# Masks of two half batches by GpSimd, their decay by one product a block, gates on SP's queue, and a new order of the work

## The chip, the cores and the metric

The kernel runs on one core of a Trainium2 chip. The time is device microseconds of one execution, as a median over runs. The engines of the core are TensorE (PE, with its weight loads PEld), VectorE (DVE), ScalarE (ACT), GpSimd (POOL) and SyncE (SP), which only issues transfers; ScalarE can issue transfers too. The transfers themselves run on 16 DMA engines that all queues share.

## The reference

Attention with a decay (a forget gate `f` for each key), then a gated FFN with a convolution of three taps. Shapes: 8 batches, 8 heads, 576 positions, 64 numbers a head; the FFN is 512 -> 1024 -> 512.

```python
scores = scale * np.matmul(q, k.transpose(0, 1, 3, 2))
cum = np.cumsum(np.log(np.clip(f, 0.0001, 1.0)), axis=-1)
decay = cum[:, :, :, None] - cum[:, :, None, :]
scores = np.where(causal, -1000000000.0, scores + decay)
attn = softmax(scores)
x = heads side by side of (attn @ v)
...
h = np.maximum(x @ w_in, 0.0)
conv_out = sum of three taps: conv_w[k] * h moved by k - 1 positions
out = (h * (1 / (1 + np.exp(-conv_out)))) @ w_out
```

## The kernel before

**Half batches.** Attention is worked off in 16 half batches `hb` of four heads, each as two pairs of heads (`i` = 2 hb + pair). Keys stand on the partitions and queries on the columns, so a score tile is a transposed block. For each half batch TensorE makes the blocks on the diagonal (`sd{i}`, 1024 columns, two heads), the blocks beside it (`so{i}.{s}`, 1024 columns, one head), and the last 64 positions of four heads (`st{hb}`, 256 columns); ScalarE takes the exponential of each (`ed`, `eo`, `et`) out of one of four PSUM tiles into fp16. Then TensorE multiplies with v (`pv{hb}.0`, `pv{hb}.1`), VectorE divides by the sums (`n`, `m`), the result is turned (`t`, `tx`), and batch b's FFN runs in eight pieces: product `f{b}.{ff}`, relu `r` on ScalarE, convolution `c` and `d` on VectorE, tanh `a` on ScalarE, gate `g` on VectorE, second product `o`, copy-out `e`, store `s`.

**Loads.** For half batches 0 and 1, q and k are loaded plainly (`ld`, L159), turned on TensorE (`tp`, L166) and copied out of PSUM with a change of the lower halves of the numbers (`cl`, L172 on ScalarE, L174 on VectorE): a float32 is read as two 16-bit rows, the upper halves are the bf16 number, and the rows of lower halves are free for other use. All other half batches are loaded with a DMA transpose (`q{hb}.{side}`, L180), from half batch 4 on into the tiles that the half batch four before it has left. v is loaded in five pieces a batch (`v{b}.{kb}`, L211, two tiles) and cast to fp16 (`va{hb}.0`, `va{hb}.1`, L219 and L221); the FFN's weights are loaded in four pieces each (`wi`, `wo`, L516) and cast (`wic`, `woc`, L524).

**Decay.** `dca` clips the gates, `dcl` takes the logarithm, `dcs` the running sum, `dck` splits it into two bf16 rows a head (`kc`, upper and lower part on partitions 0 to 63 and 64 to 127), and `ki` (L279) writes them to DRAM (`image`). The free rows of q and k then carry the decay through the same product as the scores: half batches 1 to 7 get theirs by two small row transfers (`rw{hb}`, L204 and L205), half batches 8 to 15 by a fill from `image` and a block of zeros (`fi{hb}`, L195 and L197), which also waits for `zc` (L282 to L285). Half batch 0 has no row transfer; there each block gets two further products (L315 with `sel_k`, L317 with `sel_q`).

**Causal mask.** With `MASK_PE` naming all of half batches 0 to 7, TensorE first writes the mask to a diagonal or tail tile with a product of its own (L320). For half batches 8 to 15 the exponential goes to float32 (`pd`, `p3`), and GpSimd clears the masked half on its way to fp16 (`md`, `mt`, L356 and L335).

**Order.** `ORDER` lists every step by hand; each engine, and each queue of transfers, works off its own steps in that order, and steps with a choice of engine have it behind an `@`. `add` names what a step waits for (`after`), which of a fixed number of buffers it takes and frees (`take`, `give`). The steps of SP's queue up to the second fill, in order:

```
ld0.0.0 ld0.1.0 ld0.0.1 v0.0 ld0.1.1 ld1.0.1 ld1.0.0 v0.1 v0.2 v0.3 v0.4 ki q2.1 q2.0 wi1 rw1 wi0 wi2 wi3 rw2
q3.0 q3.1 q4.1 v1.0 v1.4 v1.1 rw3 v1.3 v1.2 q4.0 q5.0 q5.1 wo3 wo1 wo0 v2.0 v2.3 v2.4 v2.1 v2.2 wo2
q6.0 q6.1 q7.0 q7.1 v3.0 v3.1 rw6 v3.2 zc v3.3 v3.4 rw7 q9.1 q8.1 q9.0 q8.0 fi9 fi8
```

The gates `f` and `conv_w` go by ScalarE's queue (L224, L226), and so do `rw4` and `rw5`.

Of the kernel before, what the change touches and what calls it, by code (L numbers as in the profile page):

```python
# [56 lines left out]
def kernel(  # L57
# [142 lines left out]
    def rows_of(hb, e="SP"):  # L200
        dma = {"SP": nc.sync, "ACT": nc.scalar}[e].dma_start
        h0 = 2 * PAIRS if hb == 0 else 0
# [1 line left out]
        dma(even_rows(hb, 0, 1, h0 * S, HS), image[0:1, 0, c, :].rearrange("j h s -> j (h s)"))  # L204
# [495 lines left out]
```

## Time and profile before

| | us |
|---|---|
| median of the runs shown (3) | 244.96 |
| lowest, highest | 244.57, 245.11 |
| the profiled execution | 244.36 |
| its span | 242.6 |

| engine | busy us | share of the span |
|---|---|---|
| TensorE | 227.2 | 94% |
| ScalarE | 207.2 | 85% |
| VectorE | 205.3 | 85% |
| GpSimd | 51.0 | 21% |

The span runs from the first to the last instruction of one profiled execution; what lies around it belongs to the time too. Busy times of different engines overlap, and matmuls are pipelined, so a single matmul's duration is longer than the step from one to the next; the chain of waits shows the steps. In a row, `out<-in` names tiles, `xN` counts instructions, and the bracket behind a timeline row tells how long the engine was idle before it and what ended that.

### The profile page before, as it was taken

What the parts mean: (1) busy time and instruction counts of PE and PEld (TensorE: products, weight loads), DVE (VectorE), ACT (ScalarE), POOL (GpSimd) and SP (SyncE); (2) the same over time, 40 slices, a digit from 0 to 9 for tenths busy, and PEclk for the clock granted to TensorE, in tenths of its full rate; (3) what the DMA queues carried; (4) which work ended last, traced back from release to release, by engine and by line L of the source; (5) the groups of instructions that cost most, each with busy time, mean ns of one, the idle gap of its engine ahead of it and who ended that gap; (6) DMA issues with size and microseconds to landing.
All of it is one profiled execution on the core that took longest, in us unless ns stands there. A gap on an engine that the chain in (4) does not pass through costs nothing.

```text
span 242.6 us, 6390 instructions
## 1 busy us (share of the span) xinstructions
PE 227.2 (94%) x2627; PEld 145.6 (60%) x2627; DVE 205.3 (85%) x324; ACT 207.2 (85%) x278; POOL 51.0 (21%) x77
## 2 busy tenths in 40 slices
...
GB/s 203 328 201 236 279 187 232 176 246 279 200 196 217 196 136 237 199 293 207 219 240 286 207 185 277 272 116 191 249 206 215 220 194 4 125 177 58 173 86 218
DMA packets 120344, 49.53 MB, mean 204 GB/s; under 512 B 109863, under 2 KB 110631, under 8 KB 120315
## 3 DMA queue, kind: packets, MB, share of 16 engines
...
HBM read 20.97 MB, written 10.17 MB: 128 GB/s over the span
## 4 chain that ended last, share of the span: by engine, by line
PE 80%; DMA 6%; DVE 5%; SPq 4%; ACT 3%; issue 1%; ACTq 0%; DVEq 0%
PE ps L474 24%; PE ps L429 21%; PE ps L312 15%; PE ps L389 7%; SPq L180 3%; PE ps L394 3%; DMA qk<-in_q_dram 3%; PE ps L166 2%; PE ps L320 2%; PE ps L414 2%; DMA qk<-image 2%; DMA pd<-in_moe_conv_w_dram 2%; PE ps L315 1%; PE ps L317 1%; DVE u L446 1%; ACT pp L370 1%
## 5 line engine op out<-in xcount | busy, mean ns | idle before, releaser
L429 PE MATMUL ps<-xt,w_in_f 128*128 128x512 f16 (+1 forms) x512 | 70.1, 286 | 0.4 <-DVE xt L417 0.4
L370 ACT ACTIVATE pp<-ps 128x1024 f16<-128x1024 f32 x64 | 64.6, 1030 | 3.5 <-PE ps L312 2.1
L474 PE MATMUL ps<-w_out_f,hg 128*128 128x512 f16 x288 | 66.7, 379 | 0.0
L312 PE MATMUL ps<-qk 128*128 128x128 bf16 (+2 forms) x576 | 63.7, 240 | 2.1 <-DMA qk<-image 1.0
L446 DVE SCALAR_TENSOR_TENSOR u<-ht,cwt 128x576 f32<-128x576 f16 x64 | 52.9, 841 | 4.4 <-ACT ht L440 4.3
L451 ACT ACTIVATE hg<-u,cw 128x576 f16<-128x576 f32 x64 | 48.6, 781 | 6.1 <-DVE u L448 6.0
L448 DVE SCALAR_TENSOR_TENSOR u<-ht,cwt,u 128x576 f32<-128x576 f16 x64 | 53.3, 846 | 0.5
L429 PEld LDWEIGHTS <-w_in_f 128*128 128x128 f16 x512 | 34.3, 98 | 28.8 <-issue 0.5
L312 PEld LDWEIGHTS <-qk 128*128 128x128 bf16 x576 | 39.4, 98 | 19.9 <-issue 4.2
L440 ACT ACTIVATE ht<-ps 128x576 f16<-128x576 f32 x64 | 40.9, 661 | 6.3 <-PE ps L429 2.8
L474 PEld LDWEIGHTS <-hg 128*128 128x128 f16 x288 | 26.9, 98 | 28.9
L458 DVE SCALAR_TENSOR_TENSOR hg<-hg,ht 128x576 f16<-128x576 f16 x51 | 38.6, 767 | 0.6 <-ACT hg L451 0.5
L356 POOL TENSOR_SCALAR_AFFINE_SELECT pp<-pd 128x1024 f16<-128x1024 f32 x16 | 19.7, 1245 | 54.0 <-ACT pd L353 54.0
L389 PE MATMUL ps<-va,pp 128*128 128x65 f16 x640 | 24.8, 193 | 1.7 <-DVE va L219 1.7
L389 PEld LDWEIGHTS <-pp 128*128 128x128 f16 x640 | 22.5, 97 | 4.2 <-DVE va L219 2.0
L405 DVE TENSOR_TENSOR xm<-ps,rc 128x896 f16<-128x896 f32 (+1 forms) x32 | 23.9, 751 | 0.5
L353 ACT ACTIVATE pp<-ps 128x1024 f16<-128x1024 f32 x16 | 16.5, 1034 | 4.8 <-PE ps L312 3.3
L353 ACT ACTIVATE pd<-ps 128x1024 f32<-128x1024 f32 x16 | 16.3, 1022 | 2.3 <-PE ps L312 1.6
L219 POOL CAST va<-vf 128x1024 f16<-128x1024 f32 x8 | 9.8, 1228 | 31.1 <-DVE xm L405 18.5
L320 PE MATMUL ps<-mask,ident 128*128 128x512 bf16 (+1 forms) x40 | 14.5, 365 | 1.3 <-ACT pp L370 0.8
L403 DVE RECIPROCAL rc<-ps 128x14 f32<-128x14 f32 (+1 forms) x32 | 6.7, 209 | 9.5 <-PE ps L394 5.8
L479 ACT COPY ob<-ps 128x1024 f32<-128x1024 f32 (+1 forms) x14 | 12.8, 918 | 0.3 <-issue 0.2
...
## 6 DMA issues: line engine op xcount, KB each, us to landing
vf<-in_v_dram SPq DMA_DIRECT2D x32, 256.0 KB
...
out_dram<-ob SPq DMA_DIRECT2D x3, 256.0 KB
```

The source lines that it names most:

```text
L312: nc.tensor.matmul(o, tk[:, h * S + k0:h * S + k0 + 128], tq[:, h * S + q0:h * S + q0 + n], start=first, stop=last and not by_matmul(hb, h))
L353: nc.scalar.activation(o, ps_of(f"sd{i}").rearrange("p (s c) -> p s c", s=2), AF.Exp, scale=SCALE)
L370: nc.scalar.activation(pair(i)[:, s, 512:1536], ps_of(f"so{i}.{s}"), AF.Exp, scale=SCALE)
L389: nc.tensor.matmul(ps[:, c:c + D + 1], block(hb, h, m, n), va[:, h, m, 0:D + 1], start=(m == 0), stop=(m == n))
L405: nc.vector.tensor_tensor(xm[:, CUT * D * u:CUT * D * u + nj * k * D].rearrange("p (j x d) -> p j x d", x=k, d=D), got[:, :, :, 0:D], r.un ...
L429: nc.tensor.matmul(ps[:, t0:t1], w_in_f16[:, cc, 128 * ff:128 * (ff + 1)], xt[:, cc // 2, x:x + t1 - t0], start=(cc == 0), stop=(cc == NCC ...
L440: nc.scalar.activation(ht_of(b, ff)[:, 2:2 + S], ps_of(f"f{b}.{ff}")[:, 0:S], AF.Relu, scale=1.0 if (b, ff) in LATE else 0.5)
L446: nc.vector.scalar_tensor_tensor(u, ht[:, 1:1 + S], cwt[:, ff, 0:1], ht[:, 2:2 + S], op0=ALU.mult, op1=ALU.add)
L448: nc.vector.scalar_tensor_tensor(u, ht[:, 3:3 + S], cwt[:, ff, 1:2], u, op0=ALU.mult, op1=ALU.add)
L451: nc.scalar.activation(hg_of(b, ff), u_t[slot[f"c{b}.{ff}", "u"]], AF.Sigmoid if (b, ff) in LATE else AF.Tanh, scale=cw[:, ff, 1:2])
L458: nc.vector.scalar_tensor_tensor(hv, hv, 1.0, ht_of(b, ff)[:, 2:2 + S], op0=ALU.add, op1=ALU.mult)
L474: nc.tensor.matmul(ps[:, 512 * j:512 * (j + 1)], w, w_out_f16[:, ff, :], start=(ff == 0), stop=(ff == NFF - 1))
```

## The change

`MASK_PE` loses half batches 0 and 1: their masks go to GpSimd as `md0` to `md3`, `mt0`, `mt1`. `PAIRS` becomes `DIRECT = 2`: for half batches 0 and 1, each block gets one further product, of a key row block `row_k` for its head with `row_q`. `row_q` holds minus the scaled running sums of batch 0's eight heads on partitions 32 to 39 (`dcq`, on POOL) and ones elsewhere; `row_k` of a head is `kc` with all rows but its own two cleared and -1 in the row of its queries (`dk0` to `dk7`, on VectorE, one for each head). `rw1` is gone. The `row_k` lie in the last two `pp` tiles and `row_q` in the last `xt` tile until these are first used; `hix` and `hfx` lie in what becomes a float32 tile of the tails.

The gates are loaded by SP (`fl`), behind `wi1`, which is now the very first transfer. Part of the constants become steps of the order: `un` (L246 and L250 of before), `zv` (clearing of `va` and `ht`), `zm` (the rows for `zc`, behind the masks since they lie in `pd`). Two exponential steps wait for `cw` or `un`, in whose buffers they write.

The order is made anew throughout, and with it the engine of 47 steps: among others the casts of `w_in` go to POOL (two), ScalarE and VectorE (one each) instead of POOL (four), those of `w_out` to VectorE instead of POOL, `va1` from POOL to VectorE; `rw4` and `rw5` go by SP, `rw3`, `rw6` and `rw7` by ScalarE. SP's steps up to the second fill are now:

```
wi1 fl ld0.0.0 ld0.0.1 ld0.1.0 ld1.0.0 ld0.1.1 ld1.0.1 v0.0 q2.0 q2.1 ki v0.2 v0.1 v0.3 v0.4 rw2 wi2 q3.0 wi0 q3.1 wi3
v1.0 v1.3 v1.1 v1.2 v1.4 q4.1 q4.0 q5.0 q5.1 v3.0 rw4 wo1 wo2 v2.0 rw5 v2.1 v2.3 wo0 wo3 q6.0 v2.2 v3.1
q6.1 q7.1 v2.4 q7.0 zc v3.3 v3.2 v4.0 q9.1 q8.1 v3.4 q8.0 v4.2 q9.0 fi8 fi9
```

TensorE's first steps are now `tp0.0.0 tp0.0.1 cw tp0.1.0 tp1.0.0 tp0.1.1 sd0` (before: `cw tp0.0.0 tp0.0.1 tp0.1.0 tp0.1.1 sd0`), and around the fills `f2.7 so14.0 o1.0 pv7.0 st7 sd16 pv7.1 o1.1 sd18` (before: `o1.1 sd18 pv7.0 sd16 pv7.1 sd19 t6 f2.7`).

```diff
-    PAIRS = 2
+    DIRECT = 2
-    MASK_PE = (0, 1, 2, 3, 4, 5, 6, 7,)
+    MASK_PE = (2, 3, 4, 5, 6, 7,)
...
+    index = cpool.tile([128, HH, SL], FP32, name="index")
+    hix, hfx = index[:, 0:2].rearrange("p h j -> p (h j)").bitcast(I32), index[:, 2:4].rearrange("p h j -> p (h j)")
+    pick = cpool.tile([128, 8], FP32, name="pick")
+    sign = cpool.tile([128, 8], FP32, name="sign")
...
+    row_k = [pp_t[NP - 1 - h // 4].bitcast(BF16).rearrange("p s c -> p (s c)")[:, 768 * (h % 4):768 * (h % 4) + 640]
+             for h in range(DIRECT * HH)]
+    row_q = xt_t[NXT - 1].bitcast(BF16)[:, 0, 0:S]
...
-    nc.scalar.dma_start(fsb, f.rearrange("b h s -> (b h) s"))
+    def load_gates():
+        nc.sync.dma_start(fsb, f.rearrange("b h s -> (b h) s"))
...
+    nc.vector.tensor_scalar(pick, hfx[:, 0:8], lit[:, 2:3], None, op0=ALU.is_equal)
+    nc.vector.tensor_scalar(sign, hfx[:, 32:40], lit[:, 0:1], -1.0, op0=ALU.is_equal, op1=ALU.mult)
...
+    def decay_q(e):
+        if e == "ACT":
+            nc.scalar.activation(row_q[32:40], cum[0:8], AF.Copy, scale=float(-1.0 / SCALE))
+        else:
+            {"POOL": nc.gpsimd, "DVE": nc.vector}[e].tensor_scalar(row_q[32:40], cum[0:8], float(-1.0 / SCALE), None, op0=ALU.mult)
+
+    def decay_k(h):
+        nc.vector.tensor_scalar(row_k[h][:, 0:S], kc, pick[:, h:h + 1], sign[:, h:h + 1], op0=ALU.mult, op1=ALU.add)
...
-        if by_matmul(hb, h):
-            nc.tensor.matmul(o[0:m], kc[:, k0:k0 + m], sel_k[:, h:h + 1].broadcast_to((128, n)),
-                             start=False, stop=False)
-            nc.tensor.matmul(o, sel_q[:, h, :], kc[:, q0:q0 + n], start=False, stop=last)
+        if own:
+            nc.tensor.matmul(o, row_k[HH * hb + h][:, k0:k0 + 128], row_q[:, q0:q0 + n], start=False, stop=last)
...
-        nc.tensor.matmul(o, ident, mask[:, 0:j].unsqueeze(1).broadcast_to((128, n, j)), start=True, stop=False)
+        nc.tensor.matmul(o, ident_b, mask[:, 0:j].unsqueeze(1).broadcast_to((128, n, j)), start=True, stop=False)
...
+    add("fl", "SP", [], load_gates)
+    add("un", "DVE", [], units)
+    early = [x for x in range(2) if x not in MASK_PE]
+    add("zm", "POOL", [f"md{2 * x + p}" for x in early for p in range(2)], levels)
+    add("zv", "POOL", [], pads)
+    add("zc", "SP", ["zm"], constants)
+    add("dca", "DVE", ["fl"], lambda: nc.vector.tensor_scalar(fsb, fsb, 1e-4, 1.0, op0=ALU.max, op1=ALU.min))
...
+    add("dcq", "POOL/ACT/DVE", ["dcs"], decay_q)
+    for h in range(DIRECT * HH):
+        add(f"dk{h}", "DVE", ["dck"], lambda h=h: decay_k(h))
...
-            if hb == 0:
-                ready = [["dck"] + [f"cl0.{p}.{side}" for side in range(2)] for p in range(2)]
+            if hb < DIRECT:
+                ready = [["dcq"] + [f"dk{HH * hb + 2 * p + s}" for s in range(2)] + [f"cl{hb}.{p}.{side}" for side in range(2)]
+                         for p in range(2)]
```

More of the change, by code (lines that the diff above doesn't have):

```diff
@@ new lines @@
+wi1 ld0 fl ld0.0.0 tp0.0.0 ld0.0.1 dca dcl dcs un dck cl0.0.0@ACT tp0.0.1 dk0 dk1 cw ld0.1.0 cwt cl0.0.1@ACT dk2 zv
+ld1 ld1.0.0 dcq@POOL tp0.1.0 dct cl0.1.0@ACT tp1.0.0 ld0.1.1 cl1.0.0@DVE tp0.1.1 dk3 cl0.1.1@ACT ld1.0.1 dk4 sd0 ed0
+tp1.0.1 tp1.1.0 v0.0 sd1 q2.0 ed1 md0 cl1.1.0@DVE so1.1 eo1.1 md1 dk7 so0.0 tp1.1.1 eo0.0 dk5 q2.1 so1.0 cl1.0.1@DVE
+so0.1 ki cl1.1.1@DVE eo1.0 v0.2 sd2 dk6 so2.1 eo0.1 st1 eo2.1 v0.1 so2.0 et1 cl2.1 v0.3 ed2 cl2.0 mt1 va0.0@POOL sd3
+st0 ed3 eo2.0 so3.1 et0 v0.4 so3.0 rw2@SP eo3.1 eo3.0 wi2 sd4 so4.0 pv0.0 md2 md3 sd5 n0.0 m0.0 q3.0 wi0 wic2@POOL mt0
@@ new lines @@
+va0.1@ACT ed5 ed4 va1.0@DVE q3.1 pv0.1 va1.1@DVE pv1.0 n0.1 wi3 pv1.1 n1.0 m0.1 m1.0 eo4.0 n1.1 t0 wic0@POOL m1.1 v1.0
+so5.1 t1 tx0@DVE wic1@ACT v1.3 tx1@DVE cl3.0 so4.1 cl3.1 v1.1 eo4.1 so5.0 eo5.1 f0.0 wic3@DVE eo5.0 r0.0 v1.2 f0.1
+r0.1 c0.0 c0.1 f0.2 f0.3 d0.0 rw3@ACT st2 h0 r0.2 et2 r0.3 f0.4 c0.2 va2.0@DVE v1.4 f0.5 r0.4 a0.0 va2.1@ACT d0.2 g0.0
+pv2.0 pv2.1 va3.0@ACT c0.4 r0.5 n2.0 st3 a0.2 d0.4 m2.0 et3 a0.4 sd6 q4.1 cl4.1 n2.1 ed6 sd7 ed7 c0.3 so7.1 c0.5 so6.0
+m2.1 q4.0 g0.2 zm eo7.1 d0.3 so6.1 so7.0 f0.6 q5.0 cl4.0 d0.5 eo6.1 eo6.0 eo7.0 q5.1 va3.1@ACT d0.1 f0.7 g0.4 pv3.0
@@ new lines @@
+v3.0 a0.5 rw4@SP cl5.0 n3.0 r0.7 a0.3 wo1 pv3.1 n3.1 t2 wo2 m3.0 v2.0 cl5.1 r0.6 m3.1 a0.1 rw5@SP c0.7 tx2@ACT sd9 t3
+tx3@DVE ed9 d0.7 g0.5 sd8 v2.1 c0.6 v2.3 f1.0 f1.1 ed8 a0.7 g0.7 g0.1 r1.0 so9.1 woc2@DVE d0.6 woc1@DVE f1.2 so9.0
+eo9.1 g0.3 r1.1 eo9.0 c1.1 f1.3 r1.2 st4 et4 so8.1 d1.1 eo8.1 sd11 sd10 wo0 ed11 r1.3 c1.0 ed10 f1.4 c1.3 st5 wo3 a0.6
+woc0@DVE et5 d1.0 f1.5 so8.0 h1 d1.3 q6.0 v2.2 g0.6 v3.1 eo8.0 a1.1 r1.5 g1.1 woc3@DVE f1.6 r1.4 c1.2 d1.2 q6.1
+va4.0@DVE f1.7 so10.1 c1.5 a1.3 g1.3 cl6.0 eo10.1 a1.0 q7.1 a1.2 o0.0 so11.1 o0.1 r1.6 g1.2 v2.4 e0.0@ACT cl6.1 r1.7
@@ new lines @@
+rw6@ACT pv4.0 c1.6 d1.5 eo11.1 va4.1@POOL c1.4 n4.0 o0.2 q7.0 m4.0 zc so11.0 cl7.1 eo11.0 va5.0@POOL o0.3 so10.0
+e0.1@ACT va5.1@POOL pv4.1 d1.4 v3.3 n4.1 sd12 m4.1 d1.6 eo10.0 sd13 cl7.0 st6 a1.4 ed12 pv5.0 v3.2 c1.7 et6 pv5.1 n5.0
+so13.1 ed13 v4.0 m5.0 n5.1 m5.1 rw7@ACT t4 t5 tx4@DVE tx5@DVE so12.0 f2.0 so12.1 d1.7 eo13.1 g1.4 a1.6 eo12.0 so13.0
+a1.7 g1.6 r2.0 eo13.0 f2.1 sd15 a1.5 q9.1 g1.0 va6.0@DVE f2.2 q8.1 g1.7 r2.1 c2.0 eo12.1 v3.4 q8.0 c2.1 r2.2 v4.2 f2.3
+f2.4 d2.0 d2.1 r2.3 pv6.0 g1.5 ed15 n6.0 h2 so15.1 a2.0 r2.4 sd14 so15.0 va6.1@DVE m6.0 c2.3 c2.4 va7.0@POOL eo15.1
@@ new lines @@
+so14.1 ed14 g2.0 pv6.1 f2.5 q9.0 eo14.1 n6.1 d2.3 d2.4 va7.1@DVE eo15.0 f2.6 fi8 f2.7 m6.1 so14.0 r2.5 c2.2 a2.4 fi9
+g2.4 a2.3 v4.3 eo14.0 r2.7 o1.0 pv7.0 g2.3 a2.1 r2.6 v4.4 st7 g2.1 c2.6 et7 n7.0 sd16 q11.0 d2.6 ed16 pv7.1 a2.6 c2.5
+n7.1 m7.0 m7.1 o1.1 c2.7 g2.6 e1.0@ACT d2.2 sd18 v4.1 t6 md16 d2.7 ed18 t7 tx6@ACT tx7@DVE sd19 a2.7 o1.2 o1.3 ed19
+s0.1 so16.0 d2.5 f3.0 g2.7 e1.1@DVE va8.0@DVE a2.5 a2.2 v5.0 q11.1 st9 eo16.0 g2.5 f3.1 r3.0 et9 r3.1 f3.2 r3.2 so18.0
+md19 eo18.0 f3.3 s1.1 v5.4 st8 va9.0@DVE c3.0 va9.1@POOL so19.0 sd17 r3.3 et8 eo19.0 c3.1 o1.4 d3.0 h3 ed17 a3.0 c3.2
@@ L19 @@
+o7.3.3 o7.3.4 g7.7 o7.4.6 o7.2.5 o7.3.5 o7.1.0 o7.4.7 o7.3.6 o7.3.7 o7.2.6 o7.2.7 o7.0.4 e7.3@DVE o7.0.5 e7.2@DVE s6.1
+o7.0.6 e7.4@ACT s5.1 o7.0.7 s7.4@ACT s7.3@SP o7.1.1 e7.0@DVE o7.1.2 o7.1.3 s7.0@SP o7.1.4 s7.2@ACT o7.1.5 o7.1.6
+o7.1.7 e7.1.1@ACT s7.1.1@SP e7.1.0@DVE s7.1.0@SP
 """
@@ L201, in rows_of @@
         dma = {"SP": nc.sync, "ACT": nc.scalar}[e].dma_start
[L202 removed]
+        h0 = 0
         c = slice(hb * HH + h0, (hb + 1) * HH)
@@ L236 @@
     nc.vector.tensor_copy(hfx, hix)
+    nc.vector.tensor_scalar(ident_b, hfx, lit[:, 0:1], None, op0=ALU.is_equal)
+    nc.vector.memset(one1, 1.0)
     nc.vector.tensor_scalar(lit[:, 3:4], lit[:, 0:1], 2.0, None, op0=ALU.is_equal)
@@ L285, in constants @@
         nc.sync.dma_start(blank, zero[0:60])
-    def warm_up(name):
-        for x in range(2):
-            nc.tensor.matmul(ps_of(name)[:, 512 * x:512 * (x + 1)], quiet[:, 0:128], quiet, start=True, stop=True)
     def conv_weights():
```

103 lines of the change are left out of this document (56 added, 47 removed).

## The prediction

> **What bounds the kernel now.** I read the page first (shares, slices), then the busy time by stretch, then the chain of waits around the one late stall, then SP's own timeline.
>
> ```profile
> span 242.6 us, 6390 instructions
> ...
> PE 227.2 (94%) x2627; PEld 145.6 (60%) x2627; DVE 205.3 (85%) x324; ACT 207.2 (85%) x278; POOL 51.0 (21%) x77
> ```
>
> TensorE is busy for 94% of the span. Where it is not shows in the stretches (start and end, length, busy us of TensorE, its weight loads, VectorE, ScalarE, GpSimd, with counts; granted clock, DMA share, GB/s):
>
> ```profile
> 0.00:26.00 26.00, 20.13 (x244) 17.04 (x245) 15.03 (x38) 16.79 (x16) 8.58 (x35) 1.00 1.00 248
> 26.00:58.00 32.00, 27.52 (x416) 19.47 (x416) 25.10 (x40) 28.25 (x39) 6.15 (x7) 1.00 1.11 228
> 58.00:107.00 49.00, 48.01 (x569) 30.65 (x567) 47.15 (x71) 46.62 (x64) 5.75 (x7) 1.00 1.04 204
> 107.00:235.00 128.00, 127.97 (x1386) 77.00 (x1387) 116.25 (x174) 114.06 (x158) 30.52 (x31) 1.00 0.81 187
> ```
>
> The DMA engines are full up to 107 (shares of 1.00 to 1.11). Idle time of TensorE is 26 - 20.13 = 5.9 us at the start, 32 - 27.52 = 4.5 us up to 58, 1.0 us up to 107 and nothing to 235; the last 4.0 us of the span are the tail (242.6 - 235 = 7.6, less the 227.2 - 223.6 = 3.6 us of busy time that these rows leave over). So an early gain reaches the end only if nothing else stands in the way before 107. One thing does:
>
> ```profile
> 94.59 6.16 DMA qk<-in_q_dram
> ...
> 102.22 4.57 DMA qk<-image
> ...
> 107.03 0.61 PE ps L312 x8
> ...
> 85.14 6.85 SPq L180 DMA_TRANSPOSE qk<-in_k_dram  x2
> 92.04 4.76 SPq L180 DMA_TRANSPOSE qk<-in_q_dram  x2
> 96.92 1.55 SPq L195 DMA_DIRECT2D qk<-blank  x2
> ```
>
> The chain ends in a transfer: half batch 8's q was issued at 94.59 and landed 6.16 us later, then `fi8` (L195, L197) filled its rows, and its last transfer landed at 102.22 + 4.57 = 106.8; `sd16` had waited for it for 1.0 us. SP's rows join end to end (85.14 + 6.85 = 91.99, next at 92.04, next at 96.92): at least here SP never waited for compute, so this date is set by the sum of what stands in its queue. TensorE and the transfers are thus within 1 us of each other at 107, and **whatever the start gains must be gained by SP's queue too**, or it becomes idle time at `sd16` and `sd18`.
>
> **The scores of half batches 0 and 1.** Masks and products, by the chain's rows (start, time, what):
>
> ```profile
> 12.99 0.19 PE ps L312
> 13.18 0.19 PE ps L315
> 13.37 0.19 PE ps L317
> ...
> 21.92 0.11 PE ps L320
> ...
> 24.27 0.22 PE ps L320
> ...
> 58.69 0.44 PE ps L312 x4
> ```
>
> Each of the three products of a block costs the same. Half batch 0 has three now, half batch 1 one; afterwards both have two, so four stand against four: nothing gained or lost. The masks go: four of 512 columns a half batch (0.22 us) and one of 256 (0.11), for two half batches 2 x 0.99 = **2.0 us of TensorE**. What the products do gain is evenness: an off-diagonal tile now takes 2 x 0.44 = 0.88 us instead of 1.32, and ScalarE needs 1.02 us for it:
>
> ```profile
> 12.94 1.02 ACT L353 ACTIVATE pp<-ps 128x1024 f16<-128x1024 f32 x1 [1.45 <-PE ps L317]
> 29.17 1.94 ACT L370 ACTIVATE pp<-ps 128x1024 f16<-128x1024 f32 x2
> ...
> L172 ACT ACTIVATE qk<-ps,lim 128x1152 uint16<-128x1152 uint16 x5 | 6.3, 1307 | 0.3 <-PE ps L166 0.3
> L332 ACT ACTIVATE pt<-ps 128x256 f16<-128x256 f32 x8 | 3.0, 387 | 0.6 <-PE ps L317 0.3 <-PE ps L312 0.2
> L534 ACT ACT_TABLE_LOAD x1 | 1.3, 1283 | 0.0
> L246 DVE TENSOR_SCALAR ident<-hfx,lit 128x128 f16<-128x128 f32 x1 | 0.7, 680 | 0.0
> ```
>
> ScalarE, which waited 1.45 us for a product before its first exponential, becomes the bound there.
>
> **The start.** The rows of now:
>
> ```profile
> 4.96 0.45 DVE L532 TENSOR_SCALAR u<-u 64x576 f32<-64x576 f32 x1 [0.69 <-DMA u<-in_f_dram]
> 8.03 0.75 DVE L274 SCALAR_TENSOR_TENSOR kc<-u,kc 64x576 bf16<-64x576 f32 x1
> ...
> 5.68 0.98 PE ps L294 x8
> 6.67 3.95 PE ps L166 x36
> 10.62 0.43 PE ps L320
> ...
> GB/s 0 0 0 0 0 0 154 100 276 353 307 392 353 246 298 327 326 298 317 292 271 265 282 353 384 392 384 384 384 407 407 376 384 372 321 288 270 236 220 218
> ```
>
> The last row is the rate of the first 12 us in 40 slices: nothing before 1.8 us, then some 340 GB/s. `wi1` (512 KB) and the gates (144 KB) now stand before q in one queue, 0.67 MB or 2.0 us. When q lands now isn't shown, at the latest 6.6; as first of its queue I put it at 4.4, so 6.4 afterwards (bounds 5.0 and 8.6). The gates move from 4.96 by 0 to 2.0 us; I take 5.6. (The Trainium skill, "DMA: Bandwidth & Descriptors", section "Queues, rings and completion order", has a DMA engine go round between the queues it has work for, packet by packet. By it the gates have a turn of their own now and lose it by this move: an estimate of 7.0, the upper bound; no row here shows it.) From there the decay takes 8.78 - 4.96 = 3.8 us as now, `un` 0.9 (0.68 by L246 and a 3x3 piece), two `dk`. A `dk` (576 elements, 2 bytes, no PSUM) is not in the trace. Bounds: a quarter of the 2304-wide row below, 0.2, and the 0.75 of L274 above; 0.3, nearest to the first, whose form it has. So 5.6 + 3.8 + 0.9 + 0.6 = 10.9. `dcq` on POOL lies beside `dck`. TensorE: 45 transposes at 3.95/36 = 0.11 plus `cw` 0.98 make 5.9, from 6.4 to 12.3; that is later than the decay, and `sd0` starts there instead of at 10.4. ScalarE turns its first block when `tp0.0.0` is done at 7.4; four of these (L172) and the table load end at 7.4 + 4 x 1.31 + 1.28 = 13.9, and from there it works off 12 exponentials of 1.02 and two tails of 0.39 without a gap: **26.9 against 31.1 now** (29.17 + 1.94).
>
> ```profile
> L186 DVE TENSOR_SCALAR qk<-qk,lim 128x2304 uint16<-128x2304 uint16 x12 | 10.1, 867 | 1.3 <-DMA qk<-in_q_dram 1.3
> ...
> L356 POOL TENSOR_SCALAR_AFFINE_SELECT pp<-pd x16: 1097/1100/1612, 106.7 to 194.5; 128x1024 f16<-128x1024 f32 x16
> ...
> L219 DVE CAST va<-vf x4: 689/692/1580, 46.6 to 198.8; 128x1024 f16<-128x1024 f32 x4
> ```
>
> GpSimd's masks (four at 1.1 us, two shorter tails) hide: `pv0.0` wants `md0` and `md1`, whose exponentials end some ten tiles earlier; `ed2`, which takes over `md0`'s buffer, comes seven tiles after it. Behind the masks on POOL stand `va0.0`, `wic2` and `wic0`, which wait for their loads anyway; for them wait `pv0.0` and the first FFN, and behind `pv0.0` on TensorE `sd5`. If the cover were gone, one mask, 1.1 us, would show. Most casts of the weights and of `va1` leave POOL: one to ScalarE (one exponential's length), six to VectorE at 0.69, in stretches where VectorE has time (25.1 busy of 32). `q4.1` now stands behind `v1`, which brings `pv2.0` forward, but `rw4` goes behind `q5.1` and `v3.0` in SP's queue, and `v3.0` waits for ScalarE's `va3.1`. Of ScalarE's 4.2 us I let 2.5 arrive at `sd9`. At the end the last two stores share SP's queue; VectorE's half of that block is ready after ScalarE's, so the first is issued by then: nothing.
>
> **SP's queue up to the fills**, the term that decides:
>
> ```profile
> 107.64 0.25 PE ps L389 x8
> 107.89 0.44 PE ps L394 x20
> ...
> 109.42 0.98 PE ps L429 x8
> ...
> DMA packets 120344, 49.53 MB, mean 204 GB/s; under 512 B 109863, under 2 KB 110631, under 8 KB 120315
> ...
> vf<-in_v_dram SPq DMA_DIRECT2D x32, 256.0 KB
> ...
> L204 SPq DMA_DIRECT2D qk<-image x5: 250/379/627, 20.5 to 83.9; - x5
> ...
> GB/s 26 116 291 291 288 291 301 131 185 53 33 47 9 193 288 289 290 293 207 117 132 195 270 289 291 289 278 157 113 83 92 51 246 290 288 293 290 146 99 173
> ```
>
> New before the last fill: `v4.0` and `v4.2`, 256 KB each, 1.3 us each at the mean rate: +2.6. Row transfers: `rw1`, `rw3`, `rw6`, `rw7` leave SP, `rw4`, `rw5` come, about 1.0 us each (0.38, and 0.6 for L205's): -2.0; the gates' issue +0.4. And the transposes: the last row is 66 to 78 us in 40 slices, where four of them follow each other; between two the rate falls from 290 to 50 to 130 GB/s for about 1 us. Of 16 before the fills 11 now follow directly on another, afterwards 6; a plain load may fill five such gaps. Bounds 0 and -3.5; I take -1.0. Sum: 0. So the later fill lands at 106.8 again. It is `fi9` then, wanted by `sd18`, and by there TensorE has done `f2.7` (0.98, L429 x8), `pv7.1` (0.25 + 0.44, L389 and L394) and `sd16` more than before `sd16` now, and `sd18`, of the same length as `sd16`, less: 1.67 us. With no idle time behind it, as now: **span 242.6 - 1.67 = 240.9.**
>
> The profiled execution took 244.36 with a span of 242.6, so 1.76 lie around it: 242.7. The median of the runs shown is 0.6 above that execution: **243.3 us**.
>
> **Rivals.**
> - *The transfers don't bind* (gaps between transposes close fully). Then the masks' 2.0 and the idle time count: 6.4 at the start and about 2.5 up to 107, against 11.4 now: 242.6 - 2.0 - 2.5 = 238.1, or **240.5**. For it: at 107 the wait is only 1.0 us. Against: SP has no gap to give.
> - *The transfers come later*: the v loads in full (+2.6), SP held at `v3.0` until `va3.1` (about 1 us), no gap closed: -2.0 + 0.4 + 2.6 + 1.0 = +2.0 on the fills, and one slow pair of transposes (6.85 us against 4.76) adds another 2. For it: nothing in the queue is idle that could make up for the v loads. Against: `v4` isn't wanted yet, and lies only two loads ahead. From a landing 1.67 us later than now the kernel is slower than before; at +4.0 the span is 244.9, or 247.3; at +3.0, which I take, **246.3**.
> - *The start is lost*: gates at 7.0, `dk` at 0.75 us each, VectorE late with `dk6` for `st1`. (The Trainium skill, "SBUF — State Buffer", section on who interferes with whom, has VectorE's casts and tensor_scalars in their fast two-port form and GpSimd lock each other out for a whole instruction; 1612 against 1100 ns in L356 and 1580 against 692 in L219 look like it.) Six masks that each hold VectorE once, by the rows' 0.5 to 0.9 us, make 3 to 5 us beside `dk` and the turned blocks; ScalarE's lead is gone, the masks' 2.0 pay for the later `sd0` (1.9): 242.5, or **244.9**, no change.
>
> **Chances.** Forecast 45%, transfers free 20%, transfers late 22%, start lost 13%. Faster than 0.2% (below 244.5; about what a measurement of this kernel can tell from no change): 0.42 + 0.20 + 0.02 = 0.64; within it 0.13; slower 0.23. The forecast's own range is 241.8 to 244.8; the whole one takes in both cases of the transfers: 239.4 to 247.2.
>
> **What would show it.** Right: TensorE's first transpose between 6 and 7.5 us and `sd0` near 12; ScalarE without idle time from 14 to 27; ten fewer L320 rows by 30 us; a TensorE wait of 1 to 4 us for `qk<-image` between 100 and 107. Wrong: no such wait and a gain over 3.5 us (transfers free), or a wait that ends after 108.5 (late); VectorE waited for at `sd2` to `st1` (start lost); idle time of TensorE after 107 (the new order, of which I priced nothing there).

## The result, and the profile after

The changed kernel is **slower**: 247.97 us median of 12 runs (245.77 to 252.41) against 244.20 us (243.07 to 248.85) measured beside it, a ratio of 1.0136 with a 95% interval of 1.0108 to 1.0165. Measured twice more, it came to 1.0228 (1.0168 to 1.0288) and 1.0217 (1.0167 to 1.0267). 243.3 us had been forecast. All ratios leave out executions more than 1.5% above the fastest of their kernel, among them the first profiled one after (250.35 us). A second one (`after_third`, 250.89 us, median there 250.09) stands beside it where the argument rests on a number.

The page of the changed kernel, span and engines:

```profile
span 248.6 us, 6379 instructions
...
PE 227.5 (91%) x2617; PEld 144.7 (58%) x2617; DVE 216.0 (87%) x344; ACT 205.3 (83%) x272; POOL 54.1 (22%) x86
```

Ten matmuls fewer, as counted, but VectorE has 10.7 us more to do. By stretch (start and end, length, busy us of TensorE, weight loads, VectorE, ScalarE, GpSimd; clock, DMA share, GB/s), first this execution:

```profile
0.00:26.00 26.00, 18.75 (x221) 15.94 (x222) 17.05 (x43) 17.99 (x18) 10.99 (x44) 1.00 0.89 230
26.00:58.00 32.00, 26.98 (x432) 19.32 (x431) 25.90 (x44) 26.81 (x38) 5.53 (x8) 1.00 1.19 222
58.00:107.00 49.00, 47.84 (x560) 30.10 (x557) 47.16 (x73) 44.09 (x59) 3.55 (x4) 1.00 1.07 203
107.00:235.00 128.00, 124.51 (x1372) 75.28 (x1370) 119.45 (x175) 112.94 (x154) 34.03 (x32) 1.00 0.90 188
```

then `after_third`:

```profile
0.00:26.00 26.00, 18.09 (x215) 15.71 (x216) 17.05 (x43) 17.18 (x17) 10.19 (x43) 1.00 0.87 222
26.00:58.00 32.00, 27.07 (x426) 18.96 (x423) 25.34 (x42) 27.10 (x39) 6.34 (x8) 1.00 1.14 218
58.00:107.00 49.00, 46.23 (x516) 29.40 (x517) 46.54 (x70) 40.75 (x54) 4.29 (x4) 0.97 1.06 219
107.00:235.00 128.00, 127.67 (x1421) 77.75 (x1419) 121.63 (x180) 116.06 (x160) 35.21 (x32) 1.00 0.87 182
```

Read the last column of the first line of each. Before, the DMA engines moved 248 GB/s in the first 26 us; now 230 and 222. Over 26 us that is 0.47 and 0.68 MB less, at the kernel's mean rate of 204 GB/s **2.3 and 3.3 us of transfers that have to be made up**. TensorE's idle time up to 107 us is 7.3 + 5.0 + 1.2 = 13.4 us here and 7.9 + 4.9 + 2.8 = 15.6 in `after_third`, against 11.4 before. The two executions lose behind the start in different places: this one waits at the fills and beyond 107 us (128 - 124.51 = 3.5 us idle), `after_third` in the stretch from 58 to 107, where the granted clock also fell to 0.97. What they have in common is the start.

The chain of waits ahead of the fills, in the first execution after (start, time, what):

```profile
89.47 0.66 PE ps L492 x4
90.13 0.81 SPq L235
...
90.99 3.84 SPq L235
...
103.18 4.74 DMA qk<-blank
107.92 0.97 issue
108.89 0.61 PE ps L377 x8
```

`sd16` waits until 108.89, 1.9 us later than before. And SP stands in this chain behind TensorE: it is released at 90.13. The same view of the kernel before, a few rows ahead of those that the prediction quoted, has the same turn:

```profile
86.40 0.45 PE ps L312 x4
86.85 0.31 SPq L180
```

So SP did wait for compute there, also before. A row of SP's timeline holds the wait as well as the issue: "85.14 6.85" was not 6.85 us of work, and rows that join end to end do not show a queue that never waits.

### The profile page after: what moved, and what is told of

Same layout as the page of the kernel before. It is cut to its first block, busy times and chain, and to the rows that moved or that the text cites. A ratio compares the mean times of both kernels' runs of the same rounds, so it can differ in the third digit from the quotient of the medians.

```text
span 248.6 us, 6379 instructions
## 1 busy us (share of the span) xinstructions
PE 227.5 (91%) x2617; PEld 144.7 (58%) x2617; DVE 216.0 (87%) x344; ACT 205.3 (83%) x272; POOL 54.1 (22%) x86
## 4 chain that ended last, share of the span: by engine, by line
PE 47%; DVE 21%; SPq 16%; DMA 10%; issue 2%; ACT 2%; DVEq 0%; ACTq 0%
PE ps L537 18%; PE ps L492 11%; SPq L235 10%; PE ps L377 8%; DMA vf<-in_v_dram 6%; DVE u L509 5%; PE ps L452 4%; DVE u L511 4%; DVE hg L521 4%; SPq L266 2%; DMA u<-in_f_dram 2%; PE ps L457 2%; DMA qk<-blank 2%; DVE qk L229 2%; DVE qk L241 2%
## 5 line engine op out<-in xcount | busy, mean ns | idle before, releaser
L433 ACT ACTIVATE pp<-ps 128x1024 f16<-128x1024 f32 x64 | 64.6, 1029 | 8.2 <-PE ps L377 6.0
L492 PE MATMUL ps<-xt,w_in_f 128*128 128x512 f16 (+1 forms) x512 | 69.2, 286 | 0.1
L377 PE MATMUL ps<-qk 128*128 128x64 bf16 (+2 forms) x576 | 64.1, 240 | 5.0 <-DMA qk<-blank 1.7
L509 DVE SCALAR_TENSOR_TENSOR u<-ht,cwt 128x576 f32<-128x576 f16 x64 | 54.8, 869 | 1.7 <-ACT ht L503 1.7
L514 ACT ACTIVATE hg<-u,cw 128x576 f16<-128x576 f32 x64 | 49.2, 779 | 8.1 <-DVE u L511 8.0
L377 PEld LDWEIGHTS <-qk 128*128 128x128 bf16 x576 | 40.2, 98 | 24.3 <-issue 5.8
L419 POOL TENSOR_SCALAR_AFFINE_SELECT pp<-pd 128x1024 f16<-128x1024 f32 x20 | 25.0, 1260 | 68.3 <-ACT pd L416 63.7
L416 ACT ACTIVATE pd<-ps 128x1024 f32<-128x1024 f32 x20 | 20.5, 1030 | 4.8 <-PE ps L377 4.1
L276 POOL CAST va<-vf 64x256 f16<-64x256 f32 x7 | 5.0, 716 | 43.7 <-DMA vf<-in_v_dram 43.7
L542 ACT COPY ob<-ps 128x1024 f32<-128x1024 f32 (+1 forms) x13 | 12.3, 945 | 2.2 <-PE ps L537 1.4
L416 ACT ACTIVATE pp<-ps 128x1024 f16<-128x1024 f32 x12 | 12.3, 1032 | 1.9 <-PE ps L377 1.5
L221 PE MATMUL ps<-ident_b,hg 128*128 128x128 bf16 x72 | 7.0, 277 | 6.7 <-DMA hg<-in_q_dram 6.7
```

The lines of the kernel that those rows point to most:

```text
L377: nc.tensor.matmul(o, tk[:, h * S + k0:h * S + k0 + 128], tq[:, h * S + q0:h * S + q0 + n], start=first, stop=last and not own)
L416: nc.scalar.activation(o, ps_of(f"sd{i}").rearrange("p (s c) -> p s c", s=2), AF.Exp, scale=SCALE)
L419: nc.gpsimd.affine_select(pair(i)[:, :, 0:512].rearrange("p s (m j) -> p s m j", j=128), pd_t[slot[f"ed{i}", "pd"]].rearrange("p s (m j) - ...
L433: nc.scalar.activation(pair(i)[:, s, 512:1536], ps_of(f"so{i}.{s}"), AF.Exp, scale=SCALE)
L492: nc.tensor.matmul(ps[:, t0:t1], w_in_f16[:, cc, 128 * ff:128 * (ff + 1)], xt[:, cc // 2, x:x + t1 - t0], start=(cc == 0), stop=(cc == NCC ...
L509: nc.vector.scalar_tensor_tensor(u, ht[:, 1:1 + S], cwt[:, ff, 0:1], ht[:, 2:2 + S], op0=ALU.mult, op1=ALU.add)
```

## The experiments

Eighteen runs followed, two of them of the changed kernel itself, each against the kernel before on the same chip (medians of before 244.18 to 244.79 us). The last column is the rate of the first 26 us in the run's profile.

| kernel | ratio to before, 95% interval | GB/s, 0 to 26 us |
|---|---|---|
| `s_alone`: new structure, old order | 0.9968 (0.9931 to 1.0005) | 260 |
| `s_first`: old start, then new order | 1.0043 (0.9999 to 1.0087) | 265 |
| `s_best`: `s_alone`, rw2 earlier | 1.0043 (1.0009 to 1.0077) | 239 |
| `s_mid`: old start, new middle, old end | 1.0083 (1.0048 to 1.0117) | 250 |
| `start_sp`: changed, first transfers in old order | 1.0112 (1.0074 to 1.0150) | 254 |
| `until_34`: new start, then old order | 1.0138 (1.0105 to 1.0171) | 227 |
| `s_rw2_act` | 1.0159 (1.0112 to 1.0205) | not used |
| `casts_pool` | 1.0171 (1.0133 to 1.0210) | 218 |
| changed, `after_third` | 1.0217 (1.0167 to 1.0267) | 222 |
| changed, `after_again` | 1.0228 (1.0168 to 1.0288) | 219 |
| `start_old` | 1.0259 (1.0221 to 1.0298) | 226 |
| `rw2_act` | 1.0261 (1.0204 to 1.0318) | 238 |
| `wi_ahead` | 1.0264 (1.0217 to 1.0312) | 244 |
| `until_107`: new up to the fills, then old order | 1.0266 (1.0237 to 1.0295) | 222 |
| `s_first_casts` | 1.0288 (1.0228 to 1.0348) | 251 |
| `s_wi_behind` | 1.0311 (1.0258 to 1.0364) | 223 |
| `order_alone`: old structure, new order | 1.0343 (1.0297 to 1.0390) | 193 |
| `sp_old` | 1.0799 (1.0749 to 1.0849) | 243 |

**Structure or order?** `s_alone` has the new scores of half batches 0 and 1 in the order of before (gates on ScalarE's queue again, the new tasks put in where their inputs are ready); `order_alone` is the kernel before in the new order. The heads of their orders:

```diff
-wi1 ld0 fl ld0.0.0 tp0.0.0 ld0.0.1 dca dcl dcs un dck cl0.0.0@ACT tp0.0.1 dk0 dk1 cw ld0.1.0 cwt cl0.0.1@ACT dk2 zv
+fl un dca cw ld0 ld1 ld0.0.0 tp0.0.0 dcl dct ld0.1.0 ld0.0.1 tp0.0.1 tp0.1.0 v0.0 ld0.1.1 ld1.0.1 ld1.0.0 dcs dcq@POOL
...
-    def load_gates():
-        nc.sync.dma_start(fsb, f.rearrange("b h s -> (b h) s"))
+    def load_gates():
+        pass
```

> The changed kernel once more, unedited, for a profile of an execution near its median. All theories: 247 to 248.5 us, about 1.012 to 1.016 of the kernel before. If the transfers decide, TensorE waits for the fills of half batches 8 and 9 between 107 and 113 us and later still (some 137 us) for the fills of 10 and 11; if VectorE decides, the chain of waits runs over VectorE without a break from about 43 to 76 us.

> The new scores of half batches 0 and 1 (GpSimd masks, one decay product a block, no row transfers for them) in the order of the kernel before, gates back on ScalarE's queue, the new small tasks put in where their inputs are ready. If the order is what costs (VectorE's casts, loads ahead of the fills): 242.5 to 244 us, 0.993 to 1.000 of before, with ten mask products fewer. If the structure itself costs (dk, decay, GpSimd holding VectorE at the start): 246 to 249 us, as the changed kernel.

> The kernel before (all masks by TensorE, decay by two more products for half batch 0, row transfers) in the new order without the new tasks; gates on ScalarE's queue as before, the row transfer of half batch 1 put behind its turned blocks. If the order is what costs: 248 to 251 us, 1.014 to 1.025 of before. If the structure costs: 244 to 245.5.

> The changed kernel with six casts (four of w_out, the last of w_in, the first of va1) back from VectorE on GpSimd, nothing else. If VectorE is the bound from 43 to 76 us: six casts of 0.60 to 0.69 us, 3.7 us off VectorE, of which 1.5 to 3 arrive: 244.8 to 246.5 us, 1.002 to 1.008 of before, and the chain of waits leaves VectorE before 60 us. If the transfers ahead of the fills decide: 247.3 to 248.3, no change against the changed kernel.

Measured: 1.0228, 0.9968, 1.0343 and 1.0171. The structure does not cost: in the old order it is 0.3% below before, with an interval that just reaches 1, and the new order is better with it than without. **The order costs.** `order_alone` is no pure test of it, since its row transfer of half batch 1 (`rw1`) was put into SP's queue by the experiment; but its timeline of SP and its stretches show very plainly what a row transfer can do at the head of that queue:

```profile
19.87 0.30 SPq L255 DMA_DIRECT2D qk<-image  x1
22.90 0.68 SPq L256 DMA_DIRECT2D qk<-image  x1
23.63 2.82 SPq L262 DMA_DIRECT2D vf<-in_v_dram  x4
```

```profile
20.00:22.00 2.00, 2.00 (x25) 1.53 (x23) 0.60 (x1) 1.63 (x2) 0.00 (x0) 1.00 0.01 3
22.00:24.00 2.00, 2.00 (x20) 1.37 (x17) 2.00 (x3) 1.02 (x1) 0.00 (x0) 1.00 0.00 0
```

From 19.87 to 22.90 SP stands at `rw1` until VectorE has turned the last block; nothing is in flight, and the DMA engines move 3 and 0 GB/s for four microseconds. `casts_pool` (four casts of w_out, one of w_in and one of `va1` back on GpSimd) fell between its two theories, and its interval overlaps that of `after_again`. Neither theory named for `after_again` shows in its trace: TensorE has no wait above 0.3 us at the fills, and the chain of waits leaves VectorE at 48.8 us and comes back to it only at 74.7.

**Where in the order?** `until_34` plays the new order up to the second turning of batch 0 and the old one from there, `until_107` up to the fill of half batch 9. `sp_old` has every transfer in the old order and the engines in the new one, but for what must wait for a load that comes later; `start_old` has this edit, and the gates on ScalarE's queue again:

```diff
-wi1 ld0 fl ld0.0.0 tp0.0.0 ld0.0.1 dca dcl dcs un dck cl0.0.0@ACT tp0.0.1 dk0 dk1 cw ld0.1.0 cwt cl0.0.1@ACT dk2 zv
-ld1 ld1.0.0 dcq@POOL tp0.1.0 dct cl0.1.0@ACT tp1.0.0 ld0.1.1 cl1.0.0@DVE tp0.1.1 dk3 cl0.1.1@ACT ld1.0.1 dk4 sd0 ed0
+ld0 fl ld0.0.0 tp0.0.0 ld0.0.1 dca dcl dcs un dck cl0.0.0@ACT tp0.0.1 dk0 dk1 cw ld0.1.0 cwt cl0.0.1@ACT dk2 zv ld1
+ld1.0.0 dcq@POOL tp0.1.0 dct cl0.1.0@ACT tp1.0.0 ld0.1.1 cl1.0.0@DVE tp0.1.1 dk3 cl0.1.1@ACT ld1.0.1 wi1 dk4 sd0 ed0
```

> The changed kernel up to the second turning of batch 0 (some 34 us), then every engine's remaining work in the order of s_alone. If the start costs (w_in and gates ahead of q, decay ready late): 247 to 249 us, 1.010 to 1.018 of before. If the order between 34 and 107 us or behind it costs: 243.5 to 245.3, 0.996 to 1.003.

> The changed kernel up to the fill of half batch 9 (some 107 us), then the remaining work in the order of s_alone. If what costs lies ahead of the fills: as the changed kernel, 1.013 to 1.023 of before. If it lies behind 107 us: as until_34. The difference of the two runs is the middle's share.

> The changed kernel with all transfers (loads, row transfers, fills, stores) in the order and on the queues of s_alone, gates on ScalarE's queue; the engines' own work in the new order, but for what has to wait for a load that now comes later. If the order of the transfers costs: 243.5 to 245.5 us, 0.996 to 1.004 of before. If VectorE's and TensorE's orders cost: 247 to 249, 1.012 to 1.020.

> The changed kernel with two edits: the first part of w_in is loaded behind the last of the first loads of q and k, and the gates are on ScalarE's queue again. If the start's two loads cost what TensorE's first row shows (first transpose at 6.7 to 7.8 us, first row before at 5.7): first transpose at 4.2 to 5.2 us, 245 to 246.5 us, 1.003 to 1.009 of before. If the start's loss is hidden later on: 247.5 to 250, no change against the changed kernel.

`until_34`, 1.0138, carries most of the loss: only its first 34 us are new. `start_old` brings TensorE's first transpose forward to 3.97 us (6.72 and 7.30 in the two executions above) and gains nothing: VectorE then waits 1.82 us, until 44.70, for a load of v of batch 1. So `w_in` and the gates ahead of q are not by themselves what costs. `sp_old` is far worse than anything else: an order of transfers belongs to the order of the engines that wait for them, and one cannot be changed alone. `until_107` is no better than the changed kernel; its seam at the fills makes a wait of its own (2.02 us for `qk<-image` at 111.02), so it says nothing on the end.

**The hole behind rw2.** In the new order SP comes to `rw2` directly behind the loads of v, and `wi2`, `wi0`, `wi3` and half batch 3 stand behind it. SP's timeline of `after_third`:

```profile
13.24 2.18 SPq L235 DMA_TRANSPOSE qk<-in_k_dram  x1
15.54 2.79 SPq L351 DMA_DIRECT2D image<-kc  x3
18.36 3.22 SPq L266 DMA_DIRECT2D vf<-in_v_dram  x4
22.92 0.30 SPq L259 DMA_DIRECT2D qk<-image  x1
23.32 0.70 SPq L260 DMA_DIRECT2D qk<-image  x1
24.08 0.41 SPq L579 DMA_DIRECT2D ob<-in_moe_w_in_dram  x1
```

VectorE's, at the same time (turned blocks, one `dk`, the clamps that rw2 wants):

```profile
18.03 2.95 DVE L229 TENSOR_SCALAR qk<-ps,lim 128x1152 uint16<-128x1152 uint16 x2
20.89 0.42 DVE L347 TENSOR_SCALAR pp<-kc,pick,sign 128x576 bf16<-128x576 bf16 x1
21.23 1.66 DVE L241 TENSOR_SCALAR qk<-qk,lim 128x2304 uint16<-128x2304 uint16 x2
```

and its stretches of two microseconds:

```profile
18.00:20.00 2.00, 2.00 (x23) 1.49 (x23) 2.00 (x3) 1.79 (x2) 1.07 (x1) 1.00 0.25 57
...
24.00:26.00 2.00, 2.00 (x32) 1.65 (x31) 0.00 (x0) 1.99 (x4) 1.62 (x3) 1.00 0.24 67
```

SP issued its last load of v by 21.58 and stands until the clamps end at 22.89. Two small row transfers go first; `wi2` is issued by 24.49, the rate is full again from 26, and from 24 to 26 us the DMA engines are a quarter used. The other hole, at 18 to 20, lies behind the small `ki` transfers that stand between half batch 2 and the loads of v. Together 1.5 + 1.5 us of full transfer are missing, about the 3.3 us that the rate of the first 26 us gave. Four kernels went for it:

```diff
 wi_ahead, in the changed kernel
-eo2.0 so3.1 et0 v0.4 so3.0 rw2@SP eo3.1 eo3.0 wi2 sd4 ...
+eo2.0 so3.1 et0 v0.4 so3.0 wi2 wi0 wi3 rw2@SP eo3.1 eo3.0 sd4 ...
 rw2_act, in the changed kernel; s_rw2_act, in s_alone
-rw2@SP
+rw2@ACT
 s_wi_behind, in s_alone
-wi0 ... wi2 ... wi3 ... rw2@SP ... q3.0 q3.1
+rw2@SP wi2 q3.0 wi0 ... q3.1 wi3
```

> The changed kernel with the loads wi2, wi0 and wi3 put in SP's queue directly ahead of rw2; nothing else. Theory of the held queue (SP stands at rw2 until VectorE has clamped half batch 2, with nothing in flight behind it: DMA share 0.09 from 24 to 26 us): no two microseconds between 20 and 30 with a share under 0.5, the bytes landed by 30 us as before or more, and 244.8 to 247 us, 1.003 to 1.011 of before. If the hole is not what costs: as the changed kernel, 1.014 to 1.023.

> The changed kernel with rw2 issued by ScalarE's queue instead of SP's, at the same place of the order. Held queue: SP goes on with wi2 and the transposes, same gain as with the three loads ahead of it, 1.003 to 1.012, unless ScalarE now stands waiting for the clamp and delays its exponentials by up to 2 us. If it is the late first part of w_in that costs rather than the hole: no gain, 1.014 to 1.023.

> s_alone (0.997 of before) with its loads wi2, wi0, wi3 and the transposes of half batch 3 put behind rw2 in the changed kernel's sequence (rw2, wi2, q3.0, wi0, q3.1, wi3). Held queue: a hole in the DMA engines' work between 20 and 27 us, 2 to 3 us lost, 1.006 to 1.016 of before. If the hole costs nothing: 0.995 to 1.001.

> s_alone with rw2 issued by ScalarE's queue behind the first off-diagonal exponential of half batch 1, so that SP goes straight from w_in to the transposes of half batch 3. In s_alone TensorE waits 2.02 us at 29.3 us for rw2's rows. Held queue: that wait is under 1 us and the transfers come 1 to 2 us earlier: 241 to 243.5 us, 0.987 to 0.996 of before. If not: as s_alone or, with ScalarE held, up to 1.005.

None of the gains came. `wi_ahead` fills the stretch, and TensorE pays for it at once:

```profile
24.00:26.00 2.00, 2.00 (x30) 1.50 (x28) 0.00 (x0) 1.99 (x3) 1.74 (x3) 1.00 1.03 321
```

```profile
30.69 0.59 PE L376 MATMUL ps<-qk 128*128 128x128 bf16 x4 [3.68 <-DMA qk<-image]
```

The second line is `sd4` in TensorE's timeline: 3.68 us of idle time stand ahead of it, which `qk<-image` ended. 1.5 MB of `w_in` now lie ahead of rw2's rows. `rw2_act` has the same wait, 2.58 us at 29.68. So **a hole is not a price by itself**; the theory in that form fell. `s_wi_behind` gave a wait that had not been meant. GpSimd's timeline:

```profile
33.87 1.04 POOL L587 CAST w_in_f<-ob 128x1024 f16<-128x1024 f32 x1 [8.31 <-DMA ob<-in_moe_w_in_dram]
34.85 1.10 POOL L419 TENSOR_SCALAR_AFFINE_SELECT pp<-pd 128x1024 f16<-128x1024 f32 x1
```

The mask `md3` stands behind the cast `wic0`, whose load was moved back, and TensorE waits for that mask:

```profile
36.00 0.84 PE L452 MATMUL ps<-va,pp 128*128 128x65 f16 x12 [7.20 <-POOL pp L419]
```

That is 7.2 us of a wait that has nothing to do with the hole; the run is no test of it. The profiled execution of `s_rw2_act` took 1302 us, its other five 247 to 249, and its trace is not used.

**Start against rest.** `s_first` is the counterpart of `until_34`: the first 34 us of `s_alone`, then the new order. `s_first_casts` is that with every cast on the engine that had it before. `s_best` moves rw2 in `s_alone`, and `after_third` is the yardstick.

```diff
 s_first_casts (the first five of twenty)
-wic3@DVE va2.1@ACT woc2@DVE woc1@DVE woc0@DVE
+wic3@POOL va2.1@POOL woc2@POOL woc1@POOL woc0@POOL
 s_best, in s_alone
-wi0 so2.0 sd3 wi2 wic0@POOL wi3 et1 mt1 eo2.0 cl2.0 cl2.1 rw2@SP n0.0 m0.0 q3.0 q3.1
+wi0 so2.0 sd3 wic0@POOL et1 mt1 eo2.0 cl2.0 cl2.1 rw2@SP n0.0 m0.0 wi2 wi3 q3.0 q3.1
```

> The first 34 us of s_alone (which was 0.997 of before), then the remaining work in the new order. If all of the loss is made in the first 34 us: 0.993 to 1.002 of before. If the new order loses by itself between 34 and 107 us (VectorE's chain from 44 to 80 us in the trace of wi_ahead, the loads of v ahead of the fills): 247 to 250 us, 1.011 to 1.024.

> s_first with every cast of the weights and of v on the engine that had it before: from 34 to 107 us VectorE loses five casts of weights (5 x 0.60 to 0.69), one of half a megabyte and two tails of v, and gains one of each. If VectorE is the bound there: 1.5 to 4 us below s_first. If the transfers are: as s_first, within 0.8 us.

> s_alone with rw2 ahead of wi2 and wi3 instead of behind them (wi1, wi0, rw2, wi2, wi3 in SP's queue): one megabyte less lies ahead of the rows for which TensorE waited 2.02 us at 29.3 us. If that wait is what keeps the masks' 2.0 us from arriving: 241 to 243 us, 0.988 to 0.995 of before, and no wait over 0.5 us at 28 to 31 us. If the transfers decide later on anyway: 0.996 to 1.001, with the wait at the fills of half batches 8 and 9 longer by what was gained.

> The changed kernel once more, unedited, as the yardstick of this chip for the other three and for the runs before it: 1.012 to 1.024 of before by all theories.

`s_first` is 1.0043 where the whole new order is 1.0217. The two differ by their first 34 us, and so do `until_34` and `s_alone`: 1.7% either way. The rest of the new order costs 0.75% (`s_first` less `s_alone`) or 0.8% (`after_third` less `until_34`). With the structure's -0.3% these make the 2.2% of `after_third`, but they must: each part is a difference of two of the same four ratios. Only `s_first` against `after_third` is a comparison on one chip. TensorE's `sd9` shows it too, in the timelines of before, `after_third` and `s_first`:

```profile
56.57 0.39 PE L320 MATMUL ps<-mask,ident 128*128 128x512 bf16 x1
```

```profile
57.46 0.38 PE L383 MATMUL ps<-mask,ident_b 128*128 128x512 bf16 x1 [1.09 <-DVE xm L468]
```

```profile
54.28 0.38 PE L383 MATMUL ps<-mask,ident_b 128*128 128x512 bf16 x1 [1.09 <-DVE xm L468]
```

With the old start it is 2.3 us early, with the new one 0.9 late. And the later fill, whose last transfer was issued at 102.22 before, at 106.69 in the first execution after, goes out in `s_first` at

```profile
101.80 0.63 SPq L251 DMA_DIRECT2D qk<-image  x1
```

`s_first_casts` gives VectorE's casts no support as the cause: with them on the engines of before, the kernel is 2.4% slower. By what is open; its TensorE waits in many places for ScalarE, and its profiled execution is its slowest. `s_best` removed the wait of `s_alone` at 29 us and was not faster. Its TensorE has new waits instead, 1.65 us until 42.53 for an exponential and 1.92 us until 44.83 for VectorE.

**SP or the engines?** `start_sp` has the first 25 transfers of the changed kernel in the order and on the queues of `s_alone`; five of TensorE's steps moved with their inputs (two turnings, and `sd4`, `so4.0` and `sd5` of half batch 2). `s_mid` joins old start, new middle and old end.

```diff
-... v0.0 sd1 q2.0 ed1 ... q2.1 ... ki ... v0.2 ... v0.1 ... v0.3 ... v0.4 ... rw2@SP ... wi2 ... q3.0 wi0 ... q3.1 ... wi3
+... v0.0 ... v0.1 sd1 v0.2 ... v0.3 ... v0.4 ... ki@SP ... q2.1 ... q2.0 ... wi1 ... wi0 ... wi2 ... wi3 rw2@SP ... q3.0 ... q3.1
```

> The changed kernel with its first 25 transfers (the loads of q, k, the gates, v of batch 0, w_in, and rw2, q2, q3) in the order and on the queues of s_alone; TensorE, VectorE, ScalarE and GpSimd keep the new order, but that three tiles of half batch 2 now wait for the later rw2. If the loss of the first 34 us is SP's order (the hole in the transfers behind rw2 and v): 6.5 MB or more landed by 26 us (5.8 in the changed kernel, 6.5 in the one before), and as s_first: 0.998 to 1.008 of before. If it is the order of the engines' work: 1.012 to 1.022.

> s_first up to the fill of half batch 9 and s_alone's order from there on: old start, new middle, old end. By the traces s_first is 1.9 us ahead of before at 115 us and loses it between 130 and 165 us, where s_alone loses nothing. If the three parts add: 241.5 to 243 us, 0.989 to 0.996 of before, faster than either kernel. If the middle's gain is not real: 0.997 to 1.005.

`start_sp` came out between its two theories, 1.0112. Its stretches:

```profile
24.00:26.00 2.00, 2.00 (x33) 1.59 (x31) 0.00 (x0) 1.99 (x3) 2.00 (x3) 1.00 1.05 371
...
0.00:26.00 26.00, 17.97 (x219) 15.20 (x220) 17.15 (x43) 17.46 (x18) 10.96 (x43) 1.00 1.03 254
```

```profile
28.78 0.38 PE L377 MATMUL ps<-qk 128*128 128x128 bf16 x4 [0.49 <-DMA qk<-image]
```

254 GB/s, and TensorE waits 0.49 us for rw2's rows, where it waited 3.68 in `wi_ahead`: with v loaded first, all of `w_in` is on its way by 22 us, before the clamps are done, and nothing has to be pushed past rw2. By the ratios about 1.0 of the start's 1.7% would be SP's order (1.0217 less 1.0112) and 0.7 the engines' own; but the changed kernel did not run on that chip, and its first measurement (1.0108 to 1.0165) is not apart from `start_sp` (1.0074 to 1.0150), so this split is not shown.

The traces give SP's order less. VectorE's cast `va2.0` of batch 1's v, in the first execution after, in `start_sp` and in `s_first`:

```profile
43.15 0.69 DVE L274 CAST va<-vf 128x1024 f16<-128x1024 f32 x1 [1.02 <-DMA vf<-in_v_dram]
```

```profile
43.31 0.68 DVE L273 CAST va<-vf 128x1024 f16<-128x1024 f32 x1
```

```profile
40.47 0.69 DVE L273 CAST va<-vf 128x1024 f16<-128x1024 f32 x1
```

In the changed kernel the cast waits for v, 1.02 us here, 0.76 in `after_third` and 0.62 in `after_again`, and the chain of waits runs back from that load over SP's queue to rw2 and the clamps. This is how the held queue reaches the engines. In `start_sp` the cast waits for no transfer and is still as late, because VectorE's first convolution, ahead of it, starts at 40.38 (39.13, 39.94 and 40.49 in the three executions after, 37.55 in `s_first`). Its `sd9` is not early either (56.91, 57.46 and 57.87 in the three executions after):

```profile
57.05 0.38 PE L383 MATMUL ps<-mask,ident_b 128*128 128x512 bf16 x1 [1.08 <-DVE xm L468]
```

So in these traces SP's order holds VectorE back by 0.6 to 1.0 us, and the engines' new order is by itself nearly as late. One thing stands out in it: the first product with v comes behind all scores of half batches 0 and 1, and VectorE is idle for 6.91 us ahead of it in the first execution after, for 5.46 in `start_sp`, for 0.97 before. No run changes that alone.

`s_mid` was to beat both kernels and did not. No kernel here is surely faster than before; `s_alone` may be.

## Why the prediction was wrong

- **Structure: right.** Ten mask products gone; a `dk` took 0.42 us (0.3 forecast, bounds 0.2 to 0.75). The row of the changed kernel's `dk`, shortest, median and longest in ns:

```profile
L347 DVE TENSOR_SCALAR pp<-kc,pick,sign x8: 413/420/507, 10.6 to 20.1; 128x576 bf16<-128x576 bf16 x8
```

- **The start's dates: right to about a microsecond.** First transpose at 6.72 (6 to 7.5 forecast; 7.30 and 7.79 in the two later executions), `sd0` at 12.9 (12.3 forecast; 13.6 there), the gates on VectorE at 6.2 (5.6 forecast). TensorE's rows:

```profile
6.72 2.10 PE L221 MATMUL ps<-ident_b,hg 128*128 128x128 bf16 x18 [6.72 <-DMA hg<-in_q_dram]
...
12.90 0.31 PE L377 MATMUL ps<-qk 128*128 128x128 bf16 x1
```

- **The lead: a size off, then gone.** ScalarE's last exponential of the two half batches ends at 28.5 in the row below, not 26.9, still 2.6 us ahead of 31.1. It did not work "without a gap": four times it waited for TensorE's products, 0.21 to 0.70 us each. "Of ScalarE's 4.2 us I let 2.5 arrive at `sd9`": none arrived (56.91 in this execution, 57.46 in `after_third`, 56.57 before). With the old start, its transfers and its order of the engines' work, 2.3 did.

```profile
26.51 1.96 ACT L433 ACTIVATE pp<-ps 128x1024 f16<-128x1024 f32 x2
```

- **The step that failed is that the sum of what stands in SP's queue dates the fills.** It was called "the term that decides" and put at 0 by adding up what SP issues: +2.6 for two loads of v, -2.0 for row transfers, +0.4, -1.0. The later fill was issued at 106.69 (104.90 in `after_third`) instead of 102.22. In `s_first`, which has those same terms and the old start, it goes out 0.4 us earlier than before, so the sum was good for what it counted. What it left out is SP waiting for the engines, on the premise that it "never waited for compute". SP stood at rw2 until VectorE's clamps were done, which the loads of batch 1's v then passed on to VectorE; and at half batch 9 TensorE released it at 90.13 instead of 86.85, which is 3.3 of the 4.5 us. SP came to that transpose at 85.88 and waited 4.3 us for TensorE; with the old start, in `s_first`, it came at 82.17 and waited 3.0.
- **"The DMA engines are full up to 107"** was not safe to carry over from the kernel before (248 GB/s): the changed one has 230 and 222. Full transfers alone would not have saved the date: `start_sp`, at 254, issues the later fill at 105.93. The diff showed where SP would stand: v behind half batch 2 and `ki`, then rw2 ahead of three loads of `w_in`. The prediction asked of `v3.0` and `va3.1` whether SP would be held, and not of rw2.
- **SP "never waited for compute": a misreading** of rows that hold wait and issue together, shown above.
- **The rivals.** The sign and roughly the time of "the transfers come later" (246.3 us) came true; its cause did not, as far as `s_first` shows: v4 ahead of the fills did not make them late. Its sign, a wait that ends after 108.5, is in the first execution (108.89) and in neither of the other two. Moving v4 alone wasn't tried. "The start is lost" had the right place, but with VectorE held by GpSimd, which in the changed kernel it is not (no `dk` over 0.51 us).
- **What lies behind 107 us** was not priced. The new order from 34 us on costs 0.75%, and part of it lies there: from 107 to 235 us TensorE is busy for 126.72 of 128 us in `s_first`, so it waits 1.3 us that the kernel before does not (0.03). In the first execution after it waits 3.5, in `after_third` 0.3. Which of the moves make these waits is open.

Open too is which of the engines' moves make the start late in `start_sp`. The parts come from kernels on different chips, where the changed kernel itself was 1.4 to 2.3%; that the two ways to the start's 1.7% agree to a tenth of a per cent is partly luck.
